# Last gate's list scatters bound one by one to TensorE's products, and two W1 pieces of the second early slot loaded and rounded during the first one

## The chip, the cores and the metric

The kernel runs on one core of one Trainium2 chip. The metric is device time in microseconds (us) of one execution. TensorE (PE) does the matrix products, and PEld is its weight load, which overlaps them; VectorE (DVE) and ScalarE (ACT) do elementwise work and empty the accumulators; GpSimd (POOL) does some copies and issues the indirect transfers; SyncE (SP) issues the plain ones. Each engine takes its own instructions strictly in order.

## The reference

A linear attention with exponential features is followed by a mixture of experts with one expert a token. A token may keep the expert of the token before it, so its expert is known only after a scan over the sequence.

```python
# attention: 8 batches, 8 heads, 576 tokens, head size 64, 128 features
proj = x @ w_phi;  proj -= max(|proj|);  phi = [exp(proj), exp(-proj)]     # for q and for k
out  = (phi_q @ (phi_k.T @ v)) / (phi_q @ sum(phi_k) + 1e-6)
# experts: E = 8, D = 512, F = 1024
logits = x @ w_gate;  local = sigmoid(x @ w_local)
e[s] = argmax(logits[s]) if s == 0 or local[s] < 0.5 else e[s-1]
y[s] = softmax(logits[s])[e[s]] * (relu(x[s] @ w1[e[s]]) @ w2[e[s]])
```

## The kernel before

**Front.** Two batches make a batch pair (NBP = 4) of 9 chunks (NC = 9) of 128 tokens. `step` handles two chunks: projections (L351), transposes (L371), the sums over keys (L403, L416), and the quotients of earlier chunks (L483). A step takes some 3.7 us on every engine. Attention rows go to `xs` in HBM, gate values to `lg` on POOL (L511 to L514).

**Gates.** After each batch pair, `gate` (a Python generator, advanced step by step) finds each token's expert and its place in the expert's list. Its chain runs DVE, PE, DVE, PE: `g_code`, a transpose (L738), a scan, `g_dg`, a small product (L750), `g_mk`, `g_cm`, `g_ci`, `g_ef`, a transpose (L767), `g_oh`, `g_ohb`, ten counting products (L780 to L785), `g_rk`, and `ri`, the row numbers. Then nine scatters (L836), one a chunk, write token number and probability into the list `lst` in HBM. The gates of pairs 0 to 2 run as `background` work, one stretch a step through `chores`; that of the last pair (`last_gate`) runs while the first products of the experts are already under way (`self.tail`).

**Early slots.** After gate 1 enough is known to choose two slots of 3 x 128 tokens of one expert (`eslots`), which can be computed before the last gate is through. `plan_early` fetches their lists (L902, read back through a transpose, L933) and `early_chores` gathers their tokens (L1223) and loads and rounds the eight weight pieces of the first slot, four of W1 and four of W2.

**Main slots.** `plan_main` needs the last gate's counts (product L942). Some 110 small DVE instructions give `p_rih` and `p_rim`, the rows of the lists to fetch; the fetches (L902, on POOL) wait until all scatters have landed. A list comes back by the transposes at L933, into `p_tokm`, and then the tokens are gathered (L1223).

**One slot.** `layer1` makes eight blocks f of hidden units, 12 products each (L1305 to L1307: a value is kept as a high and a low part, whi/wlo for weights, xhi/xlo for tokens, hh/hl for hidden values). ACT writes hh (L1358), DVE hl (L1359). `layer2` makes for each 128 tokens (a unit) eight steps f of three products, then y (L1415), and POOL scatters y to the output (L1419). `pause()` in `layer1` and the test on f in `layer2` run one entry of the list `between`: 16 places in `layer1`, two a block.

**Weights.** A piece is 512 KB. `load` has SP fetch it into one of three `wraw` buffers; `split` has ACT round it to whi (L1170) and DVE subtract for wlo (L1173), which frees the buffer. `spare()` splits the pieces beyond the newest two and loads one more; `used` calls it. So the second slot's first three pieces are fetched early, and its fourth waits until the first is split.

**What orders the work.** The code's order, run through a scheduler that may interleave each engine's instructions; a few explicit orders: `issue_after` and `here()` (behind the last product, on the issuing side), `behind_it` (a real wait on another engine's semaphore). `slots(eslots, soon, later)` takes what to run in the places of `layer1` (`soon[i]`) and `layer2` (`later[i]`) of slot i; `go` advances the last gate by one stretch.

Of the kernel before, what the change touches and what calls it, by code (L numbers as in the profile page):

```python
# [39 lines left out]
QUOTA = 16  # L40
LINE = 256

STEP = "step"

# [35 lines left out]
class Kernel:  # L82
# [9 lines left out]
    def run(self):  # L92
        nc, tc, A = self.nc, self.tc, self.A
        act, dve = self.act, self.dve
        with ExitStack() as root:
# [38 lines left out]
            n = NBP * NHP * NC  # L134
# [36 lines left out]
            plan = self.plan_main()  # L171
            go = self.advance

            def rest():
                for _ in self.last_gate:
                    if self.ranked is not None:
                        for x in self.background:
                            for _ in x:
                                pass

            def listed():
                next(plan)
                next(plan)

            def read():
# [2 lines left out]
            no = lambda: None  # L188
            m = []
# [13 lines left out]
            def singles():  # L203
                more()
                m[0]()
            self.slots(self.eslots, soon=[[no, no, no, go, no, no, go, no, no, go, rest],
                                          [no] * 9 + [read, a[0], a[1], no, a[2], no, a[3]]],
                       later=[[listed], [no, no, singles] + [lambda k=k: m[k]() for k in (1, 2, 3)] + [more]])
            back.close()
            self.mid.close()  # L210
            self.open_rest(root)
# [36 lines left out]
    def table(self):  # L248
# [8 lines left out]
        def by_three(o, x, n):  # L257
            dve.tensor_scalar(o, x, 3.0, None, ALU.is_ge)
            for k in range(2, n):
                dve.scalar_tensor_tensor(o, x, 3.0 * k, o, ALU.is_ge, ALU.add)  # L260
        yield STEP
        with self.tc.issue_after(self.last_dve.ins):
            by_three(eth, u, EARLY)
            dve.scalar_tensor_tensor(erest, eth, -3.0, u, ALU.mult, ALU.add)
        yield STEP
        with self.tc.issue_after(self.last_dve.ins):
            dve.tensor_scalar(c[11], u, 2.0, None, ALU.mult)
            dve.tensor_scalar(c[12], u, 2.0, 1.0, ALU.mult, ALU.add)
        yield STEP
        with self.tc.issue_after(self.last_dve.ins):  # L270
# [428 lines left out]
    def gate(self, bp):  # L699
# [79 lines left out]
        with self.here():  # L779
            pe.matmul(t4, self.triu, ohb, start=True, stop=False)  # L780
            for c in range(NC - 1):
                k = NC - 1 - c
# [40 lines left out]
        tc.keep_in_program_order(dve.tensor_copy(pr[:, :, 0], self.tokid[:, bp * NC:bp * NC + NC]))  # L823
        dve.tensor_mul(pr[:, :, 1], se, su)
        self.scattering = True
        for c in range(NC):
            yield STEP
            while self.tail and not self.drained:
                yield STEP
            if self.tail and self.ranked is None:  # L830
                self.late += 1
                while self.late > ROW and self.ranked is None:
                    self.held_back = True
                    yield STEP
            with self.paced():
                ins = pool.indirect_dma_start(self.lst[:, :], bass.IndirectOffsetOnAxis(ri[:, c:c + 1], 0),  # L836
                                              pr[:, c, :], None)
            if self.late > ROW:
                self.behind_it(ins, self.ranked, "it would hold the last gate's chain")
            tc.declare_no_dep(ins.ins, group="scatter", reason="scattered rows are distinct")  # L840
            tc.add_to_no_dep_group("scatter", ins.ins)
            self.scattered.append(ins)
# [543 lines left out]
    def layer2(self, s, between, held=None):  # L1386
        tc, dve, pool = self.tc, self.dve, self.pool
        hh, hl = s["h"]
        self.need(s, 8) if len(s["ei"]) == 1 else None
        for k in range(s["n"]):  # L1390
            if hasattr(self, "psr"):
                t = self.psr.tile([128, DM], F32, name="l2")
            else:
                t = self.psb.tile([128, DM], F32, name="l2", tag="nm")
            m = min(128, s.get("cols", s["n"] * 128) - k * 128)
            o = slice(k * 128, k * 128 + m)
            for f in range(8):
                c = slice((f % 2) * DM, (f % 2) * DM + DM)
                self.both(s, 4 + f // 2, t[0:m], hh[:, f, o], hl[:, f, o], c, f == 0, f == 7)
                if f in ((0, 2) if s["n"] > 1 else (1, 3, 5)) and between:  # L1400
                    between.pop(0)()
                if f % 2 and k == s["n"] - 1:
                    self.used(1)
                elif f % 2:
                    self.spare()
            last = held is not None and k == s["n"] - 1
            y = self.mx2.tile([128, DM], F32, name="yl", bufs=1) if last else self.mx2.tile([128, DM], F32, name="y")
            u = s["u"] + k
            if last:
                w = s["prob"][0:m, u:u + 1]  # L1410
                self.act.activation(y[0:m], t[0:m], AF.Copy, scale=w)
            elif hasattr(self, "psr"):
                self.marks[dve] = dve.tensor_scalar_mul(y[0:m], t[0:m], s["prob"][0:m, u:u + 1])  # L1413
            else:
                self.marks[self.act] = self.act.activation(y[0:m], t[0:m], AF.Copy, scale=s["prob"][0:m, u:u + 1])  # L1415
                self.last_y = self.marks[self.act]

            def put(y=y[0:m], at=s["tok"][0:m, u:u + 1]):
                ins = pool.indirect_dma_start(self.A["out"], bass.IndirectOffsetOnAxis(at, 0), y, None,  # L1419
                                              bounds_check=NT - 1, oob_is_err=False)  # L1420
                tc.declare_no_dep(ins.ins, group="outs", reason="each token is written once")
                tc.add_to_no_dep_group("outs", ins.ins)
            if last:
                held.append(put)
            else:
                put()

    def slots(self, order, held=None, soon=(), later=()):
# [19 lines left out]
        for i, s in enumerate(order):  # L1448
            while s.get("asked", len(s.get("w", ()))) < 8:
                self.spare()  # L1450
            self.need(s, 4)
            new = order[i + 1] if i + 1 < len(order) else None
            rows = self.tokens(ahead[i], bool(soon) and i == 0, self.last_y if held is not None and i == 0 else None)
            first, rest = list(soon[i]) if i < len(soon) else [], rows
            if not soon and s["n"] > 1:
                some = [f for u in rows for f in u[0:3]]
                first = [lambda: None] * 16
                for k, f in enumerate(some):
                    first[1 + k * 15 // len(some)] = f
                rest = [u[3] for u in rows]  # L1460
            if not soon:
                rest += [lambda x=x, k=k: self.gather_x(x, k) for x in ahead[i + 1] for k in range(x["n"])]
            if len(s["ei"]) == 1:
                self.layer1(s, first)
            else:
                self.layer1_two(s, [])
            if i < len(later):
                rest = list(later[i]) + rest
            self.layer2(s, rest, None if new else held)
            for f in rest:  # L1470
                f()
            s.clear()
# [131 lines left out]
```

## Time and profile before

| | |
|---|---|
| median of 3 runs | 715.51 us (713.83 to 719.53) |
| the profiled execution | 712.14 us, of which span 710.3 us |
| PE busy | 698.4 us, 98% of the span |
| PEld busy | 617.9 us, 87% |
| DVE / ACT / POOL busy | 460.7 / 411.8 / 265.0 us |
| granted TensorE clock, mean | 0.997 |
| mean DMA traffic | 176 GB/s |

The span is the time from the first to the last instruction of the profiled execution; 1.9 us lie around it. Busy times are averages over stages: the front (to 276 us), the first early slot (276 to 312 us), the second (312 to 348 us) and the main slots (from 348 us). In a timeline row the figures are start, duration, engine, line, operation, and in brackets how long the engine was idle before it and what released it.

### The profile page before, as it was taken

How to read it: one execution, taken by the hardware profiler on the slowest of the kernel's cores; microseconds unless marked ns; L12 is line 12 of the kernel's file. 1: busy time of each engine (PE TensorE's matmuls, PEld its weight loads, DVE VectorE, ACT ScalarE, POOL GpSimd, SP SyncE). 2: the span in 40 equal slices, each digit the busy share in tenths (PEclk: the TensorE clock that was granted, in tenths of full speed). 3: DMA queues.
4: the chain of work that ended last, by engine and by line, in shares of the span. 5: the costliest groups of instructions: out<-in, count | busy, mean ns of one | idle time of the engine just before them, and what ended most of it. 6: DMA issues, size and time to landing. Idle time of an engine off the chain costs nothing. (4 is left out here: it accounts for less than half of the span.)

```text
span 710.3 us, 22974 instructions
## 1 busy us (share of the span) xinstructions
PE 698.4 (98%) x9576; PEld 617.9 (87%) x9576; DVE 460.7 (65%) x876; ACT 411.8 (58%) x888; POOL 265.0 (37%) x532
## 2 busy tenths in 40 slices
PE   7999999999999999999999999999999999999996
PEld 6999999999999999888887986889888877888985
DVE  6898899889998995683537446535643367554522
ACT  5777776777768873434465654745754269471512
POOL 0211101430146675562345551345744236443311
PEclk9999999999999999999999999999999999999998
DMA  7855545555466863254818975344886375444200
GB/s 232 268 154 148 160 124 155 148 149 161 134 183 198 252 189 113 64 181 129 280 70 294 405 279 194 135 149 150 265 307 252 110 243 172 150 163 155 76 27 31
DMA packets 66074, 125.17 MB, mean 176 GB/s; under 512 B 7180, under 2 KB 45260, under 8 KB 65910
## 3 DMA queue, kind: packets, MB, share of 16 engines
q1 hardware_dynamic: 57680, 100.90, 44.8%
q0 software_dynamic: 7968, 22.58, 9.0%
q8 instruction: 76, 1.25, 0.7%
q14 instruction: 30, 0.25, 0.1%
q10 hardware_dynamic: 320, 0.20, 0.1%
HBM read 102.11 MB, written 21.80 MB: 174 GB/s over the span
## 5 line engine op out<-in xcount | busy, mean ns | idle before, releaser
L1173 DVE TENSOR_TENSOR wlo<-wraw,whi 128x1024 fp32r<-128x1024 f32 x80 | 96.4, 1222 | 37.8 <-ACT whi L1170 37.5
L1305 PE MATMUL l<-whi,hh 128*128 128x512 f32 (+1 forms) x288 | 113.4, 394 | 0.5 <-ACT hh L1358 0.5
L1306 PE MATMUL l<-wlo,hh 128*128 128x512 f32 (+1 forms) x288 | 112.7, 391 | 0.8 <-DVE wlo L1173 0.8
L1307 PE MATMUL l<-whi,hl 128*128 128x512 f32 (+1 forms) x288 | 112.6, 391 | 0.0
L362 ACT ACTIVATE kp<-sb 128x512 f32<-128x512 f32 x144 | 83.3, 623 | 48.9 <-DVE sb L359 48.1
L1359 DVE SCALAR_TENSOR_TENSOR hl<-l,hh 128x512 fp32r<-128x512 f32 (+3 forms) x84 | 50.4, 600 | 93.2 <-ACT hh L1358 93.1
L1170 ACT CAST whi<-wraw 128x1024 fp32r<-128x1024 f32 x80 | 82.4, 1047 | 43.8 <-PE l L1307 27.0
L1358 ACT ACTIVATE hh<-l 128x512 fp32r<-128x512 f32 (+3 forms) x84 | 44.0, 525 | 108.9 <-PE l L1307 57.2
L1305 PE MATMUL l<-xhi,whi 128*128 128x384 f32 (+4 forms) x308 | 106.8, 347 | 0.0
L1307 PE MATMUL l<-xhi,wlo 128*128 128x384 f32 (+4 forms) x308 | 106.5, 346 | 0.0
L1306 PE MATMUL l<-xlo,whi 128*128 128x384 f32 (+4 forms) x308 | 106.4, 345 | 0.0
L358 DVE TENSOR_REDUCE m<-pj 128x8 f32<-128x1024 f32 (+1 forms) x74 | 88.3, 1193 | 20.4 <-PE pj L351 18.3
L1285 POOL COPY xg<-z 32x128 f32<-32x128 f32 x208 | 70.4, 339 | 58.7 <-DVE z L1273 41.4
L359 DVE TENSOR_TENSOR sb<-pj,m 128x1024 f32<-128x1024 f32 (+1 forms) x74 | 88.5, 1196 | 5.6
L351 PE MATMUL pj<-first,kq 64*128 64x128 f32 x1152 | 85.3, 289 | 3.5 <-DMA first<-in_first 3.4
L483 PE MATMUL nm<-kvs,qp 128*64 128x73 f32 x2304 | 86.3, 227 | 0.5 <-issue 0.4
L1419 POOL DMA_INDIRECT out<-y,p_tokm x31 | 37.4, 1205 | 127.2 <-DVE y L1413 126.0
L386 ACT ACTIVATE qp<-pj 128x512 f32<-128x512 f32 x144 | 78.1, 596 | 8.4 <-PE pj L371 7.5
L483 PEld LDWEIGHTS nm<-kvs,qp 128*64 128x64 f32 x2304 | 79.1, 137 | 1.0 <-issue 0.7
L351 PEld LDWEIGHTS pj<-first,kq 64*128 64x128 f32 x1152 | 71.4, 190 | 9.4 <-DMA first<-in_first 3.4
L403 PE MATMUL kvp<-v,kp 128*64 128x65 f32 x2048 | 75.3, 224 | 0.1
L1285 ACT COPY xg<-z 32x128 f32<-32x128 f32 x208 | 61.7, 296 | 20.3 <-DVE z L1273 16.0
(266 smaller groups left out, 1080.0 us busy)
## 6 DMA issues: line engine op xcount, KB each, us to landing
wraw<-in_w1h SPq DMA_DIRECT2D x44, 512.0 KB, 5.1
wraw<-in_w2h SPq DMA_DIRECT2D x44, 512.0 KB, 5.6
kq<-in_kqT SPq DMA_DIRECT2D x47, 384.0 KB, 4.1
v<-in_va SPq DMA_DIRECT2D x48, 195.0 KB, 3.5
xs<-xo SPq DMA_DIRECT2D x48, 128.0 KB, 2.4
whi<-in_w1h SPq DMA_DIRECT2D x8, 512.0 KB, 5.8
wlo<-in_w1h SPq DMA_DIRECT2D x8, 512.0 KB, 8.6
whi<-in_w2h SPq DMA_DIRECT2D x8, 512.0 KB, 7.2
```

The lines of the kernel that those rows point to most:

```text
L351: self.last_pe = self.pe.matmul((q if j else t)[:, h, i % 2, j, :], kq[r, j, s], self.w2[r], start=True, stop=True)
L358: dve.tensor_reduce(m[:, a:a + n], x[:, s], AX.X, ALU.max, apply_absolute_value=True)
L359: self.last_dve = dve.tensor_sub(to[:, s], x[:, s], m[:, a:a + n].unsqueeze(2).broadcast_to([128, n, 128]))
L362: self.last_act = act.activation(kp[:, :, :, sg, :].rearrange("p c h f -> p h c f"), sb[:, :, :, 0], AF.Exp, scale=1.0 - 2 * sg)
L386: self.act.activation(qp[:, sg].rearrange("p h (c r k) -> p (h c) r k", c=2, r=2), src, AF.Exp, scale=1.0 - 2 * sg)
L483: self.last_num = self.pe.matmul(e["t"][r, c - c0, k], self.ch[i]["qp"][:, sg, h, q0 + r.start:q0 + r.stop], kvs[:, sg, k], start=sg == 0, ...
L1170: self.act.copy(hi, raw)
L1173: (low or self.dve).tensor_sub(lo[:, c], raw[:, c], hi.bitcast(F32)[:, c])
L1285: self.marks[engine] = copy(to[q, :, g], z[g, :, b, :])
L1305: mm(o, ah, bh, start=first, stop=False)
L1306: mm(o, ah, bl, start=False, stop=False)
L1307: self.last_pe = mm(o, al, bh, start=False, stop=last)
```

## The change

In this section and in the prediction c0 to c8 are the nine scatters of the last gate.

- `gate` yields a new mark `LIST` ahead of the last gate's scatters. In the front, gates 0 to 2 issue two scatters a step and not one.
- `rest`, which ran the remainder of the last gate and all open scatters in one go in the 11th place of the first early slot's `layer1`, is replaced by `row`: one stretch or one scatter a call. Six calls stand in the last six places of that `layer1` (from block 5 on), five more in its `layer2`: `row` is called in unit 0 at f = 0 (`plan_row`), 4, 6 and in unit 1 at f = 4, 6. Five scatters of gate 2 that are still open at the end of the front run freely as before.
- Each of c0 to c8 waits for PE's last product as of its place (`behind_it(ins, self.last_pe, ...)`).
- The first two places of `layer1` call `spare` (load a piece), and the sixth `landed(1)`: the first two W1 pieces of the second early slot are split there, behind block 2, and not after block 7.
- In the front the order moves as well: on PE the early lists' transposes (L933) stand four steps earlier, and gate 2's L750, L767 and L780 one step earlier each, so that they follow its L738 step by step, as those of gates 0 and 1 do.
- `layer2` of the first early slot has places at f = 0, 2, 4, 6 (before: 0, 2). The plan's first part stands where it was; its second part, the fetches, is called (`listed`) after unit 1 and not together with the first.

```diff
-STEP = "step"
+STEP, LIST = "step", "list"
...
-            def rest():
-                for _ in self.last_gate:
-                    if self.ranked is not None:
-                        for x in self.background:
-                            for _ in x:
-                                pass
+            def lists():
+                for x in self.last_gate:
+                    if x is LIST:
+                        break
+                for x in self.background + [self.last_gate]:
+                    for _ in x:
+                        yield
+            flow = lists()
+
+            def row():
+                next(flow, None)
+
+            def plan_row():
+                next(plan)
+                row()
 
             def listed():
-                next(plan)
+                for _ in flow:
+                    pass
                 next(plan)
...
-            self.slots(self.eslots, soon=[[no, no, no, go, no, no, go, no, no, go, rest],
+            self.slots(self.eslots, soon=[[self.spare, self.spare, no, go, no, lambda: self.landed(1), go, no, no, go] + [row] * 6,
                                           [no] * 9 + [read, a[0], a[1], no, a[2], no, a[3]]],
-                       later=[[listed], [no, no, singles] + [lambda k=k: m[k]() for k in (1, 2, 3)] + [more]])
+                       later=[[plan_row, 0, row, row, 1, 2, row, row, listed], [no, no, singles] + [lambda k=k: m[k]() for k in (1, 2, 3)] + [more]])
...
+        if self.tail:
+            yield LIST
         for c in range(NC):
-            yield STEP
+            if self.tail or c % 2 == 0:
+                yield STEP
...
+            if self.ranked is not None:
+                self.behind_it(ins, self.last_pe, "the list's rows are written one transfer after the other")
...
-                if f in ((0, 2) if s["n"] > 1 else (1, 3, 5)) and between:
+                if f in ((1, 3, 5) if s["n"] == 1 else (0, 2, 4, 6) if s is self.eslots[0] else (0, 2)) and between:
...
-                rest = list(later[i]) + rest
+                rest = [x if callable(x) else rest[x] for x in later[i]]
```

What stands on DVE in the middle of the last gate's chain, between `g_cm` and `g_ef`, during the first early slot's `layer1`, before:

```order
L78 TENSOR_REDUCE g_cm<-g_mk 9x1
L78 TENSOR_SCALAR g_ci<-g_sc,g_cm 9x128
L78 TENSOR_SCALAR g_ci<-g_ci 9x128
L78 CAST g_ef<-g_ci 9x128
L1359 SCALAR_TENSOR_TENSOR hl<-l_6342,hh 128x384
```

And now (the line numbers are those of the changed file; wlo is at L1188, hl at L1374):

```order
L78 TENSOR_REDUCE g_cm<-g_mk 9x1
L1188 TENSOR_TENSOR wlo<-wraw,whi 128x1024 x2
L78 TENSOR_SCALAR g_ci<-g_sc,g_cm 9x128
L1374 SCALAR_TENSOR_TENSOR hl<-l_6363,hh 128x384
L78 TENSOR_SCALAR g_ci<-g_ci 9x128
L78 CAST g_ef<-g_ci 9x128
L1374 SCALAR_TENSOR_TENSOR hl<-l_6391,hh 128x384
```

The two subtractions of the moved pieces and one hl come ahead of `g_ef`; on ACT their two roundings stand between the hh of blocks 2 and 3.

The place on PE where `g_ef` is read (`pt<-first,g_ef`), between blocks 4 and 5 of the same `layer1`, before:

```order
L1307 MATMUL l_6370<-xhi,wlo 128x384
L767 MATMUL pt<-first,g_ef 128x9
L1305 MATMUL l_6393<-xhi,whi 128x384
L1306 MATMUL l_6393<-xlo,whi 128x384
L1307 MATMUL l_6393<-xhi,wlo 128x384
```

And now:

```order
L1322 MATMUL l_6391<-xhi,wlo 128x384
L1320 MATMUL l_6414<-xhi,whi 128x384
L1321 MATMUL l_6414<-xlo,whi 128x384
L1322 MATMUL l_6414<-xhi,wlo 128x384
L1320 MATMUL l_6414<-xhi,whi 128x384
L1321 MATMUL l_6414<-xlo,whi 128x384
L777 MATMUL pt<-first,g_ef 128x9
L1322 MATMUL l_6414<-xhi,wlo 128x384
```

The transpose has moved five products back; the counting products that follow it stand three products later than before. Nothing else differs on PE from there to the end of the program.

POOL's queue from the first early slot's `layer1` to the fetch of the main list (`lr<-lst,p_rim`), before (`p_rih` are two small fetches of half lists):

```order
L836 DMA lst<-pr,ri 36992x16 x17
L1419 DMA out<-y,p_toke 4608x512
L902 DMA lr<-lst,p_rih_6651 4x1024
L902 DMA lr<-lst,p_rih_6669 4x1024
L1419 DMA out<-y,p_toke 4608x512 x2
L902 DMA lr<-lst,p_rim 30x2048
```

And now:

```order
L849 DMA lst<-pr,ri 36992x16 x13
L1434 DMA out<-y,p_toke 4608x512
L849 DMA lst<-pr,ri 36992x16
L917 DMA lr<-lst,p_rih_6762 4x1024
L1434 DMA out<-y,p_toke 4608x512
L917 DMA lr<-lst,p_rih_6780 4x1024
L917 DMA lr<-lst,p_rim 30x2048
L1434 DMA out<-y,p_toke 4608x512
```

Three scatters have gone to the front; the output of unit 0 now stands ahead of the last scatter, and the main fetch ahead of the output of unit 2.

## Rows read from the trace of the kernel before

**Rows 1.** The page, busy time of PE: us, share of the span, instructions

```profile
PE 698.4 (98%) x9576; PEld 617.9 (87%) x9576; DVE 460.7 (65%) x876; ACT 411.8 (58%) x888; POOL 265.0 (37%) x532
```

**Rows 2.** What PE waited for: us in total, times, longest

```profile
PE pj L351 <- DMA first<-in_first: 3.4, 1, 3.4
PE l L1306 <- DVE wlo L1173: 0.8, 1, 0.8
PE l L1305 <- ACT hh L1358: 0.5, 1, 0.5
```

**Rows 3.** Stretches: us, busy (instructions) of PE, PEld, DVE, ACT, POOL; clock; DMA share, GB/s

```profile
275.87:293.84 17.97, 17.97 (x112) 17.16 (x111) 10.56 (x43) 3.60 (x8) 9.03 (x13) 1.00 0.09 23
293.84:312.00 18.16, 18.16 (x87) 14.73 (x86) 17.04 (x92) 9.28 (x12) 14.81 (x12) 1.00 0.47 142
312.00:329.80 17.80, 17.80 (x102) 17.42 (x101) 7.05 (x33) 4.42 (x10) 6.23 (x7) 1.00 0.40 129
```

**Rows 4.** Timeline of DVE: gate 1, last gate, then split and plan (start, duration)

```profile
176.64 0.21 DVE L78 CAST g_ef<-g_ci 9x128 f32<-9x128 int32 x1
...
283.90 0.15 DVE L78 TENSOR_REDUCE g_cm<-g_mk 9x1 f32<-9x9 f32 x1
284.64 0.22 DVE L78 CAST g_ef<-g_ci 9x128 f32<-9x128 int32 x1
285.49 0.56 DVE L1359 SCALAR_TENSOR_TENSOR hl<-l,hh 128x384 fp32r<-128x384 f32 x1 [0.63 <-ACT hh L1358]
...
295.50 1.23 DVE L1173 TENSOR_TENSOR wlo<-wraw,whi 128x1024 fp32r<-128x1024 f32 x1
296.79 1.21 DVE L1173 TENSOR_TENSOR wlo<-wraw,whi 128x1024 fp32r<-128x1024 f32 x1
...
314.90 0.14 DVE L78 TENSOR_SCALAR p_rim<-p_rowm 54x1 int32<-54x1 f32 x1
```

**Rows 5.** Timeline of PE: gate 1; last gate; last scatter's product; list read

```profile
176.91 0.22 PE L767 MATMUL pj<-first,g_ef 9*128 9x9 f32 x1
...
286.95 0.22 PE L767 MATMUL pt<-first,g_ef 9*128 9x9 f32 x1
288.62 0.21 PE L780 MATMUL pt<-g_ohb,consts 128*128 128x72 bf16 x1
...
304.27 0.39 PE L1307 MATMUL l<-whi,hl 128*128 128x512 f32 x1
...
322.52 0.41 PE L933 MATMUL pt<-first,lr 34*128 34x34 f32 x2
```

**Rows 6.** Timeline of ACT: hh of block 2; two roundings in a row

```profile
282.54 0.49 ACT L1358 ACTIVATE hh<-l 128x384 fp32r<-128x384 f32 x1 [1.71 <-PE l L1307]
...
294.43 1.98 ACT L1170 CAST whi<-wraw 128x1024 fp32r<-128x1024 f32 x2
```

**Rows 7.** Timeline of SP: issue of the second early slot's second W1 piece

```profile
265.12 0.35 SPq L1157 DMA_DIRECT2D wraw<-in_w1h  x1
```

**Rows 8.** The page, DMA issues: count, KB each, median us to landing

```profile
wraw<-in_w1h SPq DMA_DIRECT2D x44, 512.0 KB, 5.1
```

**Rows 9.** Timeline of POOL: scatters, an output, fetches

```profile
289.61 0.96 POOL L836 DMA_INDIRECT lst<-pr,ri  x1 [5.42 <-DVE pr L78]
...
304.19 0.96 POOL L836 DMA_INDIRECT lst<-pr,ri  x1 [0.31 <-DMA lst<-pr,ri]
305.45 3.55 POOL L1419 DMA_INDIRECT out<-y,p_toke  x1 [0.30 <-issue]
310.52 1.86 POOL L902 DMA_INDIRECT lr<-lst,p_rih  x1 [0.31 <-issue]
316.32 0.92 POOL L902 DMA_INDIRECT lr<-lst,p_rim  x1 [0.31 <-issue]
```

**Rows 10.** Tile lst, its transfers (scatters among them)

```profile
DMA to landing us min/median/max: 2.1/3.6/5.3
```

**Rows 11.** Tile lr, its transfers (the fetched lists)

```profile
DMA to landing us min/median/max: 4.0/5.0/5.3
```

## The prediction, made before the changed kernel ran

> **What bounds the kernel now.** I read the page's busy times first: PE works 98% of the span [rows 1]. Then what PE waited for. The reader is to see how little there is: 3.4 us for the first inputs, before any work, 0.8 us for one wlo and 0.5 us for one hh, both in main slots [rows 2]. None of the three waits lies in the two early slots, which the change rearranges. Then the stretches: in the first slot's layer 1 (275.87 to 293.84), its layer 2 (to 312.00) and the second slot's layer 1 (to 329.80) PE is busy in every microsecond, at a granted clock of 1.00 [rows 3]. So in the region of the change an edit can gain nothing unless it shortens PE's own work, and PE has the same products in both programs. It can lose, wherever something PE reads comes later than PE does.
>
> [...]
>
> **The change, part by part.**
>
> *Front: two scatters a step, gate 2's chain a step earlier.* The same 36 scatters are issued, three more of them ahead of the early slots; POOL is busy 37% [rows 1]. On PE gate 2's L750, L767 and L780 now follow L738 in consecutive steps, and on DVE `g_mk` to `g_ef` interleave with rc and xo. This is how gates 0 and 1 stand in the kernel before. Gate 1 prices it: `g_ef` ends at 176.64 + 0.21 = 176.85 and L767 starts at 176.91 [rows 4, 5]; it fits by 0.06 us, and PE's list has no wait there. Cost 0; as upper bound, one further short DVE instruction in the way, 0.2 us.
>
> *Two pieces split in the first slot's layer 1.* The second piece is issued by SP at 265.12 [rows 7] and lands some 5.1 us later [rows 8], at 270, so the data are there. ACT: hh of block 2 ends at 282.54 + 0.49 = 283.03, the two roundings take 1.98 us [rows 6] and end at 285.0. DVE: the first wlo can start when the first rounding ends, 284.05, which is also when `g_cm` ends (283.90 + 0.15); the second starts 1.29 later and takes 1.21 [rows 4], so DVE is back at the gate's chain at 284.05 + 1.29 + 1.21 = 286.55. From `g_cm`'s end to `g_ef`'s end it took 284.86 - 284.05 = 0.81 before; now one hl (0.56 [rows 4]) stands in between: `g_ef` ends at 286.55 + 0.81 + 0.56 = 287.92 if nothing overlaps, at 287.4 if hl hides in the chain's own latencies. PE reads it at L767: before at 286.95 [rows 5]; now five products later, 5 x 0.175 = 0.87, at 287.82. A tie: between 0.4 us early and 0.1 late. Before, `g_ef` was 2.1 us early: that cover is used up, and every further 0.1 us on DVE is 0.1 us of PE. I take 0.1; as upper bound hl once more, 0.7. The counting products stand 3 products later than before, 288.62 + 0.52 = 289.14, 1.32 behind L767 where there were 1.67 [rows 5]; but the hl that stood between `g_oh` and `g_ohb` now precedes them, which gives 0.56 back against 0.35. Cost 0.
>
> What the moved split frees: the fourth and fifth pieces can be fetched from about 286 and not 297 (the first wlo of before starts at 295.50), in a stretch where the DMA engines are 9% busy [rows 3]. The list of waits shows no PE wait for these pieces, so no gain. DVE has two wlo (2 x 1.21) fewer between counts and `p_rim`, which so comes at about 314.90 + 0.14 - 2.4 = 312.6.
>
> *Scatters bound to PE.* Before, POOL sat idle 5.42 us until the last gate's DVE chain released it at 289.61 [rows 9]. That chain moves with L780 by 0.5 us, and one hl (0.56) now stands ahead of `ri`: c0 leaves at about 290.7, say 291. Scatters follow every 1.27 us at POOL's own pace (0.96 and 0.31 of idle [rows 9]), so c7 leaves at 291 + 7 x 1.27 = 299.9, and each of c0 to c7 later than the product it waits for: the binding decides nothing for them. The output of unit 0 comes next, at 299.9 + 1.27 = 301.2, and is done by 302 or, at the longest one seen (3.55 [rows 9]), by 305. c8 waits for the third product of unit 1, f = 4, which ends at 304.27 + 0.39 = 304.66 [rows 5]. So c8 leaves at 304.7, half a microsecond after the last scatter of before (304.19 [rows 9]). That is where the binding decides, and the only place.
>
> Behind c8 on POOL: the two half-list fetches with the output of unit 1 between them, then the main fetch. c8 lands 3.6 us after issue [rows 10], 308.3; fetch 0.92, output about 1, fetch 0.92 with 0.3 between [rows 9] end at 312.0; then `p_rim`: the main fetch leaves at 312.6 and not at 316.32 [rows 9], and lands 5.0 us later [rows 11] at 317.6. PE reads it at 322.52 [rows 5]: 4.9 us early, where it was 1.2 us early before (316.32 + 5.0 = 321.3). Cost 0, gain 0, but a wider margin.
>
> One row speaks for the slower end: outputs and fetches took 3.55 and 1.86 us on POOL at 305.45 and 310.52 [rows 9], against 0.92 at 316.32. [...]
>
> *Extra places, `plan_row`, `listed` apart from it.* No instruction is added to PE; the plan's DVE instructions are the same. Cost 0.
>
> **Sum.** 0 to 0.1 + 0.1 + 0 = +0.1 us on the profiled execution: 712.14 to 712.2. The median of before lies 3.4 us above its profiled execution (715.51); the forecast is for the median: **715.5 us**.
>
> **Rivals.**
> 1. *The runs that aren't profiled lose what the profile shows as a thin margin.* The list was only 1.2 us early, and the executions spread over 713.83 to 719.53. If the 3.4 us between profile and median are PE waiting at L933 for a late list, the wider margin gives them back: 715.5 - 3.4 = 712.1. For it: the margin. Against: nothing in the trace shows such a wait. 12%.
> 2. *The bound scatters make the list late (slower).* c8 waits behind PE and the output ahead of it, and what follows takes its longest times: c8 at 305.1 (301.2 + 3.55 + 0.3), landing 5.3 [rows 10] at 310.4, then fetch 1.86, output 3.55, fetch 1.86 and three gaps of 0.3: main fetch at 318.6, landing 5.3 [rows 11] at 323.9. PE waits 1.4 us at L933: 716.9. It decides from the moment the main fetch leaves later than 322.5 - 5.3 = 317.2. To pass 1% it would have to leave 7.2 us later than that. 8%.
> 3. *DVE reaches `g_ef` late*, up to 0.7 us: 716.2. It is the tie above, at its far end. 12%; it is within the same verdict.
> 4. *The change does not do what it says*: the binding only forbids what POOL's pace forbids anyway. Then nothing moves but the wlo pair: 715.5, the same time as the forecast; counted with it.
>
> **How the numbers follow.** The forecast (nothing but PE's tie, at most +0.1) has 65%, rivals 1, 2 and 3 have 12, 8 and 12%, and 3% are left for what I don't see. A measurement of this kernel can tell about 1% (7.2 us) from no change; all named cases lie within that. The range takes rival 1 at its low end (712.1, less half a microsecond: 711.5) and, at the high end, the highest run of before (719.53), since rivals 2 and 3 add only 1.4 us to the median and single runs scatter by more: 711.5 to 719.5. Faster by over 1% would need 7.2 us out of PE waits that total under 6 in the whole profile: 2%. Slower by over 1%: 4%. Within 1%: 94%.
>
> **What would show it.** In the profile after: PE's waits in the main slots are still some 0.8 us for a wlo and 0.5 us for an hh; L767 of the last gate starts within 0.3 us of `g_ef`'s end; c0 to c7 follow each other at 1.27 us, and only c8 waits for PE; the main fetch leaves near 312.6. Rival 2 shows as a PE wait at L933 for `lr`, rival 3 as one at L767 for `g_ef`. The prediction would be wrong if PE shows a new wait of several microseconds in the two early slots, or if the main slots, whose order is the same, lose or gain time.

## The result, and the profile after

The changed kernel took 721.83 us (median of 14 runs, 719.60 to 725.84) and the kernel before, beside it, 717.37 (14 runs, 713.83 to 721.14): ratio 1.0064, 95% interval 1.0048 to 1.0081, 4.5 us slower. Forecast were 715.5 us, in a range of 711.5 to 719.5, and no change. Of the 6.3 us by which that was missed, 1.9 lie in the kernel before, which took 717.37 us here and 715.51 in the three runs that the forecast started from; 4.5 lie in the change. The profiled execution of the changed kernel took 721.97 us, of which span 720.1, at a mean granted clock of 0.999.

One thing has to be known to read the numbers below. The effect found here depends on the measurement, not on the program alone: of the measurements in which the changed kernel or its decisive part ran, three show it (the first sort) and two don't (the second), whole sets of runs at a time, and one chip showed it once and on another occasion, by the time of the kernel before (the pairs themselves did not run there), was of the second sort. Each comparison is therefore made within one measurement, whose kernel before is named with it; A is the one above, B to G follow.

The page, busy time of the engines (answers to [rows 1]), and PE's waits, longest first (answers to [rows 2]):

```profile
PE 704.3 (98%) x9576; PEld 620.9 (86%) x9576; DVE 460.5 (64%) x876; ACT 411.8 (57%) x888; POOL 263.6 (37%) x535
```

```profile
PE pj L361 <- DMA first<-in_first: 3.4, 1, 3.4
PE kvp L413 <- issue: 1.5, 5, 0.4
PE l L1320 <- ACT hh L1373: 1.1, 1, 1.1
PE pj L381 <- issue: 0.8, 2, 0.4
PE l L1321 <- DVE wlo L1188: 0.8, 1, 0.8
PE pj L469 <- issue: 0.5, 1, 0.5
PE pj L361 <- issue: 0.5, 2, 0.3
```

New are the lines with "issue": PE stood still although nothing that the profile shows was missing. They lie at L361, L381, L413 and L469, which are lines of the front (L351, L371, L403 and L459 before). The share of busy time, 98% in both programs, hides them. The lines name some 3.3 us of standing still; PE's busy time grew by 5.9 us besides, for the same 9576 products. The ends of products are modelled, so that a part of each stop is booked as work: 32 products at L413 that take 1.15 us without a stop (trace of D below) stand here as 0.52 us for 9 and 0.86 for 22.

Where the time goes: line up the two programs product by product and read how much later each starts. At 126 us the changed kernel is 0.3 us late, after gate 0's pairs of scatters (144.3 us) 3.3, after gate 1's (218 us) 7.5, after gate 2's two pairs (277 us) 9.1, and behind the last gate's rearrangement (289.5 us) 9.2; at 363 us it is still 9.2. So the part that the prediction worked out at length cost nothing, and the part that it priced at nothing cost nearly everything. (The two profiled executions stand 9.8 us apart, the medians 4.5: the one of before, 712.14, is quicker than every run of before in this measurement.)

The front at close range, in stretches of 4 us (behind the length: busy us and instructions of PE, PEld, DVE, ACT and POOL, then granted clock, DMA share, GB/s). Before:

```profile
130.00:134.00 4.00, 4.00 (x114) 3.85 (x112) 3.77 (x6) 2.72 (x7) 1.68 (x4) 1.00 0.64 188
134.00:138.00 4.00, 4.00 (x115) 3.85 (x112) 3.32 (x7) 3.32 (x9) 1.69 (x5) 1.00 0.45 128
```

After:

```profile
130.00:134.00 4.00, 3.59 (x88) 3.34 (x88) 2.85 (x5) 1.85 (x4) 2.39 (x7) 1.00 0.51 154
134.00:138.00 4.00, 3.76 (x92) 3.51 (x90) 3.07 (x5) 2.42 (x8) 2.59 (x6) 1.00 0.49 135
```

PE gets through 180 products where it did 229. Timeline of POOL in the changed kernel, two steps, scatters only:

```profile
128.00 1.07 POOL L849 DMA_INDIRECT lst<-pr,ri  x1 [0.69 <-issue]
...
129.44 1.02 POOL L849 DMA_INDIRECT lst<-pr,ri  x1 [0.17 <-issue]
...
132.54 1.00 POOL L849 DMA_INDIRECT lst<-pr,ri  x1
...
133.90 0.98 POOL L849 DMA_INDIRECT lst<-pr,ri  x1 [0.16 <-issue]
```

Timeline of PE beside it, the sums over keys only:

```profile
129.90 0.52 PE L413 MATMUL kvp<-v,kp 128*64 128x65 f32 x9
130.82 0.86 PE L413 MATMUL kvp<-v,kp 128*64 128x65 f32 x22 [0.41 <-issue]
...
134.27 0.76 PE L413 MATMUL kvp<-v,kp 128*64 128x65 f32 x11
135.28 0.84 PE L413 MATMUL kvp<-v,kp 128*64 128x65 f32 x21 [0.24 <-issue]
```

The second scatter runs from 129.44 to 130.46, PE goes dry after its ninth product and resumes at 130.82; the next one runs from 133.90 to 134.88, PE goes dry after the eleventh and resumes at 135.28. PE comes back some 0.4 us behind the end of the second scatter, in the middle of a series, at no border of a tile; no operand can have been what it waited for: kp was written 1.19 us before the product at 130.82 began, and 0.62 us before the one at 135.28. Behind the first scatter of a step there is no stop.

### The profile page after: what moved, and what is told of

Read it like the earlier page. It is cut to its first block, busy times and chain, and to the rows that moved or that the text cites. A ratio compares the mean times of both kernels' runs of the same rounds, so it can differ in the third digit from the quotient of the medians.

```text
span 720.1 us, 22985 instructions
## 1 busy us (share of the span) xinstructions
PE 704.3 (98%) x9576; PEld 620.9 (86%) x9576; DVE 460.5 (64%) x876; ACT 411.8 (57%) x888; POOL 263.6 (37%) x535
## 5 line engine op out<-in xcount | busy, mean ns | idle before, releaser
L1188 DVE TENSOR_TENSOR wlo<-wraw,whi 128x1024 fp32r<-128x1024 f32 x80 | 96.2, 1221 | 38.4 <-ACT whi L1185 37.7
L1374 DVE SCALAR_TENSOR_TENSOR hl<-l,hh 128x512 fp32r<-128x512 f32 (+3 forms) x84 | 50.4, 600 | 93.5 <-ACT hh L1373 91.8
L361 PE MATMUL pj<-first,kq 64*128 64x128 f32 x1152 | 86.4, 289 | 4.0 <-DMA first<-in_first 3.4
L361 PEld LDWEIGHTS pj<-first,kq 64*128 64x128 f32 x1152 | 72.1, 191 | 10.2 <-DMA first<-in_first 3.4
L413 PE MATMUL kvp<-v,kp 128*64 128x65 f32 x2048 | 78.2, 225 | 1.9 <-issue 1.5
```

The source lines that it names most:

```text
L361: self.last_pe = self.pe.matmul((q if j else t)[:, h, i % 2, j, :], kq[r, j, s], self.w2[r], start=True, stop=True)
L1188: (low or self.dve).tensor_sub(lo[:, c], raw[:, c], hi.bitcast(F32)[:, c])
```

## Experiments

**B. The parts, each alone** (kernel before: 712.72 us in this measurement). `e1_one_a_step` is the changed kernel without the pairs, `e2_pairs_only` the kernel before with the pairs and nothing else:

```diff
 e1   for c in range(NC):
-         if self.tail or c % 2 == 0:
-             yield STEP
+         yield STEP
 e2   for c in range(NC):
-         yield STEP
+         if self.tail or c % 2 == 0:
+             yield STEP
```

> The changed kernel with one scatter a step in the front, as before; the moved split of the two W1 pieces and the binding of the last gate's scatters stay. Theory A (the loss sits in the front's steps with two scatters, 12 such steps by some 0.65 us of stopped PE in the profile): ratio to the kernel before 0.998 to 1.002, and in its trace no PE idle put down to issue between 125 and 265 us. Theory B (the loss comes from the early slots, where the split moved and the scatters were bound): ratio 1.005 to 1.008, as with the whole change.

> The kernel before with one edit alone: two scatters a step in the front, one right behind the other. Theory A: all of the loss is back, ratio 1.004 to 1.009, with PE idle put down to issue in the steps with two scatters (12 of them). Theory B: ratio 0.998 to 1.002.

Measured: 712.84 us, ratio 1.0002 (0.9988 to 1.0016), and 713.14 us, 1.0006 (0.9989 to 1.0022). The rest is free, as expected, but so were the pairs, which theory A put at 1.004 to 1.009. In the trace of the pairs the second scatters follow as closely as in the changed kernel (130.02 behind 128.58) and PE doesn't stop. Theory A fell in this form, for this measurement. (The pairs in the front are ten, not twelve as expected: five of gate 2's scatters stay behind for the early slots.)

`e3_pairs_spaced` lets the second scatter of a step wait for the step's first kp, which sets seven of the ten pairs apart (the first pair and gate 2's two stay 1.4 us from start to start); `e4_pool_busy` puts POOL arithmetic behind each single scatter of the kernel before:

```diff
 e3   with self.paced(late=c % 2 == 1):      # tick reads kp instead of m
 e4   ins = pool.indirect_dma_start(self.lst[:, :], ...)
+     if not self.tail:
+         x = self.w2[:, 0:116].unsqueeze(1).broadcast_to([128, 3, 116])
+         with tc.issue_after(ins.ins):
+             pool.tensor_add(w, x, x)
```

> The changed kernel, still two scatters in a step of the front, but the second one is released by the step's first kp (ACT) and not by m (DVE): it leaves some 1.9 us behind the first, with about 0.8 us of free time on POOL between them, where the pair had 0.35. Theory A1 (PE is stopped because the second scatter follows the first too closely): most of the loss goes, ratio 0.998 to 1.003, PE idle by issue at most 1 us in the front. Theory A2 (what counts is how many list rows are written in a step): the loss stays, ratio 1.004 to 1.008. Theory A3 (a scatter that runs into the products of 64 or 128 columns stops PE wherever it stands): the loss stays or grows.

> The kernel before, one scatter a step, and right behind each of the 27 scatters of the front one POOL addition of 128x348 elements (about 1 us, no transfer; its result is read by nobody). Theory A4 (the issuing of descriptors by a second scatter stops PE): nothing, ratio 0.998 to 1.002. Theory A5 (POOL at work in SBUF for some 2 us on end stops PE, whatever the work): 27 stops of some 0.6 us, 16 us, ratio 1.015 to 1.025.

Measured: 1.0000 (0.9983 to 1.0017), and 714.71 us, 1.0035 (1.0017 to 1.0052). The first tells nothing where pairs are free anyway. Of the 27 additions expected, 19 run in the front, as eight of gate 2's scatters are issued behind it. 2.0 us for 19 additions of 0.78 us, 0.10 each, is no stop of 0.6 us; by the trace gate 0's nine cost nothing, and the loss lies in gate 1's stretch. But as pairs were free here, it tells only that the additions themselves are nearly so.

**C. The changed kernel again, and larger doses** (kernel before: 715.72 us). `e5_extra_scatter` puts a second scatter of the same rows behind each one that runs in the front, into a list that nobody reads (19 of them, not 27 as expected); `e6_nine_in_a_step` is the changed kernel with a gate's nine scatters in one step:

```diff
 e5   ins = pool.indirect_dma_start(self.lst[:, :], ...)
+     if not self.tail:
+         with tc.issue_after(ins.ins):
+             more = pool.indirect_dma_start(self.lst2[:, :], ...)
 e6   for c in range(NC):
-         if self.tail or c % 2 == 0:
+         if self.tail or c == 0:
              yield STEP
```

> The changed kernel itself, once more. The pairs alone cost nothing (1.0006) and neither does the rest alone (1.0002). Theory P (the two parts together cost it, though each alone is free): ratio 1.004 to 1.009 and PE idle by issue in the steps with two scatters, 0.2 to 0.5 us each. Theory C (the stopped PE belongs to the loading and the chip of that measurement, not to the program): ratio 0.998 to 1.002, no PE idle by issue in those steps.

> The kernel before, and behind each of the 27 scatters of the front a second one of the same 128 rows into a list that nobody reads. If two scatters on end stop PE, there are now 27 such places in 27 steps: at 0.65 us each 17.5 us, ratio 1.02 to 1.03. If two on end are free, as the pairs alone were: 0.998 to 1.003.

> The changed kernel with all nine scatters of a gate in one step of the front, some 12 us of POOL on end. If PE is stopped while a second and later scatter is issued: 8 stops a gate, 24 in all, 0.65 to 1.3 us each, 16 to 31 us, ratio 1.022 to 1.044. If scatters on end are free for PE: only the additions to lg stand behind them on POOL, and xo's buffers come free late; ratio 1.000 to 1.010.

Measured: 722.76 us, 1.0107 (1.0085 to 1.0129); 733.56 us, 1.0244 (1.0225 to 1.0263); 747.69 us, 1.0431 (1.0409 to 1.0453). Here the stops are back, and they grow with the dose. By the first one's expectation, that spoke for theory P; its ratio lies even above the 1.004 to 1.009 named for it. Ten pairs cost 7.04 us, 0.70 each; 19 extra scatters 17.84, 0.94 each. That 17.5 had been expected is no support for 0.65 us a pair: it came of 27 scatters, and the agreement is chance. With nine on end each of the 24 further ones costs 31.97 / 24 = 1.33 us. Nine on end, in stretches of 3 us (behind the length: PE, PEld, DVE, ACT and POOL, busy us and instructions; granted clock, DMA share, GB/s):

```profile
127.00:130.00 3.00, 3.00 (x86) 2.85 (x86) 2.67 (x5) 2.17 (x7) 1.66 (x4) 1.00 0.54 159
130.00:133.00 3.00, 1.84 (x33) 1.39 (x29) 0.00 (x0) 0.31 (x1) 2.55 (x5) 1.00 0.23 70
133.00:136.00 3.00, 1.31 (x14) 0.70 (x14) 2.45 (x2) 0.00 (x0) 2.67 (x5) 1.00 0.46 134
136.00:139.00 3.00, 0.84 (x6) 0.63 (x6) 0.00 (x0) 2.39 (x5) 2.67 (x5) 0.54 0.05 11
```

And PE's timeline in it, where the scatters follow every 1.34 us:

```profile
131.53 0.36 PE L413 MATMUL kvp<-v,kp 128*64 128x65 f32 x5 [0.43 <-issue]
132.28 0.39 PE L413 MATMUL kvp<-v,kp 128*64 128x65 f32 x5 [0.39 <-issue]
133.02 0.38 PE L413 MATMUL kvp<-v,kp 128*64 128x65 f32 x5 [0.36 <-issue]
133.77 0.35 PE L413 MATMUL kvp<-v,kp 128*64 128x65 f32 x4 [0.37 <-issue]
```

PE advances by four or five products at a time, then has nothing. From 86 products in 3 us it comes down to 33, 14 and 6, and DVE and ACT, which work on what it makes, are busy in one of these three stretches each (but for 0.31 us). So PE goes on, at 53 products in 9 us, and the price of 1.33 us for a scatter every 1.34 us holds more than these stops. Among it are the products that follow the fall of the granted clock, to 0.54 in the last of these stretches and to 0.50 in the next (139 to 142 us): 16 of them take 1.16 us at a granted clock of 1.00 (L361, row of 129.12 in the same trace) and 2.08 behind that stretch:

```profile
143.52 2.08 PE L361 MATMUL pj<-first,kq 64*128 64x128 f32 x16
```

**D. All on one chip** (kernel before: 712.88 us), to tell a matter of the measurement from a joint effect of the two parts:

> The changed kernel again, beside its parts on the same chip. Theory C (whether a second scatter on end stops PE is a matter of the chip or of how the program was loaded): either all kernels with pairs are slower together, 1.004 to 1.012, or none is, 0.998 to 1.002. Theory P (the pairs cost only together with the rest of the change): this one 1.004 to 1.012, the pairs alone 0.998 to 1.002.

> Pairs alone, on the same chip as the changed kernel. Theory C: the same ratio as the changed kernel within 0.003. Theory P: 0.998 to 1.002 whatever the changed kernel shows.

> The pair with its second scatter released by kp. Where the changed kernel is slower by 0.4% or more: if the short distance is what stops PE, 0.998 to 1.003; if it is the second scatter as such, the changed kernel's ratio within 0.003. Where the changed kernel is not slower: 0.998 to 1.002, and nothing is told.

> One scatter a step with the rest of the change. By either theory 0.998 to 1.002; if the moved split or the binding costs something that the first chip hid, 1.003 or more.

Measured: 0.9998 (0.9982 to 1.0013), 1.0005 (0.9988 to 1.0021), 1.0012 (0.9997 to 1.0028), 1.0000 (0.9985 to 1.0015). None is slower, the whole change included. That speaks for theory C and against P, by which the whole change is slower wherever it runs. The same two steps in the changed kernel here, POOL's scatters:

```profile
129.63 1.07 POOL L849 DMA_INDIRECT lst<-pr,ri  x1 [0.69 <-issue]
...
131.07 1.02 POOL L849 DMA_INDIRECT lst<-pr,ri  x1 [0.17 <-issue]
...
132.92 1.00 POOL L849 DMA_INDIRECT lst<-pr,ri  x1
...
134.28 0.98 POOL L849 DMA_INDIRECT lst<-pr,ri  x1 [0.16 <-issue]
```

and PE's sums over keys:

```profile
131.52 1.15 PE L413 MATMUL kvp<-v,kp 128*64 128x65 f32 x32
...
135.21 1.13 PE L413 MATMUL kvp<-v,kp 128*64 128x65 f32 x32
```

The same program, the same scatters at the same distance and of the same length, and 32 products in one piece. Lined up with C's trace of the same program, C falls back by 0.8 to 1.3 us in each of the ten steps with a pair, 9.5 us, and by 0.6 us in all the time between; that is about the difference of the two medians, 722.76 and 712.77. A's trace, lined up with D's, falls back by 8.4 us in the ten steps. The kernel before stands 2.8 us higher in C as well, which is why C's ratio shows 7.0 us and not 10: the ratios, 0.45 to 0.70 us a pair, understate what a pair costs PE.

**E. Pairs alone and the rest alone where pairs stop PE** (kernel before: 716.05 us; nine in a step beside them show the stops):

> Pairs alone, on another chip. If this chip is of the kind on which scatters on end stop PE (nine in a step near 1.043 beside this run): 1.004 to 1.011, all of the change's loss, and PE idle by issue in the steps with two scatters. If the loss needs the rest of the change as well: 0.998 to 1.002 even there. On a chip of the other kind: 0.998 to 1.002.

> The rest of the change alone, one scatter a step. If the pairs are all of the loss: 0.998 to 1.002 on either kind of chip. If the moved split or the binding has a share in it: 1.003 to 1.008 on a chip on which nine in a step are slow.

> Nine scatters in one step, with the changed kernel's rest. On a chip on which scatters on end stop PE: 1.035 to 1.045, as before. On one of the other kind: 1.000 to 1.005 if it does not feel them at all; 1.010 to 1.030 if it only has a larger reserve, which two on end do not use up and nine do.

Measured: pairs alone 722.50 us, 1.0093 (1.0076 to 1.0109); the rest alone 713.05 us, 0.9955 (0.9939 to 0.9971); nine in a step 745.49 us, 1.0418 (1.0399 to 1.0436). This settles the part: ten pairs cost 6.45 us, 0.65 each, and the rest costs nothing; it came out 3.0 us quicker, below the 0.998 to 1.002 expected. Lined up with the trace of pairs alone in D, this one falls back by 8.6 us in the ten steps. By theory P the pairs alone would have been free, so P falls here. The trace of the pairs shows the stops at the same places:

```profile
129.50 0.48 PE L403 MATMUL kvp<-v,kp 128*64 128x65 f32 x8
130.35 0.88 PE L403 MATMUL kvp<-v,kp 128*64 128x65 f32 x23 [0.36 <-issue]
```

and the trace of the rest alone has no idle time by issue at all between 125 and 225 us, where the kernels with pairs have 2.7, 3.3 and 2.6 us in A, C and E (no kernel has more than 0.2 us there in the other measurements). That holds for the scatters into the list alone. Between 225 and 275 us, where gathers and subtractions on POOL stand beside them, traces of either sort with one or two scatters a step have idle time by issue as well, up to 1.3 us (spaced pairs in D, 229.76 us), and the profile of before has 0.29 us at 266.59 us beside a single scatter. What causes these is not shown.

**F and G. What is left** (kernel before: 713.01 and 712.81 us). `e7_rest_unbound` is one scatter a step with the rest of the change, without the line that binds c0 to c8 to a product:

```diff
-     if self.ranked is not None:
-         self.behind_it(ins, self.last_pe, ...)
```

> The kernel before, for its profile on this chip. Ratio 0.998 to 1.002. On a chip of the first kind (median near 716): its trace shows some 3 us of PE idle put down to issue that the profile of before shown here (712.14) does not have, either beside single scatters and fetches in the front (before 265 us) or in the two early slots. On the other kind (median near 712.8): nothing new.

> One scatter a step, the moved split and the later list as in the rest of the change, but no scatter bound to a product of PE: the last gate's scatters leave at POOL's own pace. On a chip of the first kind: 0.994 to 0.997 if the moved split gains the 3 us, 0.999 to 1.002 if the binding gains them. On the other kind: 0.998 to 1.002.

> The changed kernel with the second scatter of a step released by kp, some 0.8 us of free time on POOL between the two. On a chip of the first kind (kernel before near 716): if the short distance stops PE, the time of one scatter a step, 0.994 to 1.001, and no PE idle by issue at the second scatters; if two in a step are too many wherever they stand, 1.006 to 1.012. On the other kind (before near 713): 0.998 to 1.002.

> One scatter a step with the rest of the change. On a chip of the first kind: 0.994 to 0.997 if the gain seen there once is the program's, 0.998 to 1.002 if it was chance. On the other kind: 0.998 to 1.002.

Measured in F: the kernel before against itself 0.9976 (0.9954 to 0.9997), without the binding 1.0003 (0.9986 to 1.0020). In G, on the chip of E: spaced pairs 1.0003 (0.9989 to 1.0018), one a step 1.0000 (0.9984 to 1.0017). By the kernel before, near 713 us, both are of the sort of B and D, so neither question of them was answered: the spaced pair was never measured where close pairs stop PE, and the 0.9955 of the rest alone was not seen again (1.0002, 1.0000 and 1.0000 in the other three). A kernel that came out at 0.9976 against itself, below the 0.998 expected, says what a quarter of a per cent is worth here.

## Why the prediction was wrong, step by step

**The step that failed** is "Front: two scatters a step, gate 2's chain a step earlier", its "Cost 0; as upper bound, one further short DVE instruction in the way, 0.2 us". Measured: 4.5 us in A, 7.0 in C and, for the pairs alone, 6.45 in E, at 0.45 to 0.70 us a pair against the kernel before, and 0.6 to 1.3 us a pair where two traces are lined up; and nothing in B and D. The wait that the upper bound had in view, PE behind gate 2's `g_ef`, came at 0.4 us in C (L777) and 0.5 in E (L767) and not at all in A: twice the bound, and still a small part. It failed in its reasoning and not only in its size. The cover named was POOL's 37% of busy time, a share of the span, which says that POOL has room and nothing of what a POOL instruction does to PE meanwhile. The price was taken from gate 1's chain on DVE [rows 4, 5], which is another question. No row of the trace had two scatters on end beside products that take 0.035 us each (32 in 1.13 us), so by the prediction's own rule the cost was unknown, and neither bound was worked out from a row of a scatter.

**What the trace could not have told.** The profile of before was of an execution of 712.14 us, below the lowest of its own three runs (713.83). The prediction saw the 3.4 us between that and the median, and made a rival of it. Measurements in which pairs stop PE have the kernel before at 717.4, 715.7 and 716.1 us, the others at 712.7 to 713.0: by its time the profile belongs to the second sort, where pairs are free.

A second sign says the same, and it needs no pairs. A trace also records when semaphores change. Of the changes that engines make while POOL issues an indirect transfer, 19 to 30% are missing in each of the seven traces of A, C and E, that of the rest alone (75 of 359), where PE does not stop, among them, and 1 to 3% in the other thirteen, the profile of before included (8 of 387). So the condition belongs to the measurement and is there with one scatter a step too. Whether the recording has a part in stopping PE, or only loses records for the same reason, was not tested.

What costs the kernel before, which has no pairs, those 3 us isn't shown: no profile of it from a measurement of the first sort exists. The nearest is the trace of `e5_extra_scatter` in C, which has its order in the early slots, with twelve scatters on end from 306.57 to 322.10 us. There PE stops by issue and then waits for hl and for the list (L940 is L933 of before):

```profile
PE l L1312 <- DVE hl L1366: 1.0, 1, 1.0
PE pt L940 <- DMA lr<-lst,p_rim: 0.5, 1, 0.5
PE l L1312 <- issue: 0.4, 1, 0.4
```

Lined up with the trace of the kernel before in F, it falls back by 2.9 us between 320 and 343 us, near the 2.8 us by which the kernel before is slower in C. Scatters bound one by one never stood more than seven on end (the rest alone in E), which would fit that run's gain of 3.0 us. This is argued from one trace, not shown.

**The split of two pieces in the first slot: right.** Counting the 9.2 us by which all is later here, `g_ef` was to end at 296.6 to 297.1 and L777 (L767 before) to start at 297.0 (five products later, at 0.175 us a product, that is 17.80 us for 102 in [rows 3]). DVE's timeline, then PE's:

```profile
296.42 0.22 DVE L78 CAST g_ef<-g_ci 9x128 f32<-9x128 int32 x1
```

```profile
296.98 0.22 PE L777 MATMUL pt<-first,g_ef 9*128 9x9 f32 x1
```

`g_ef` ends at 296.64, 0.3 us ahead: the early end of the tie. The stretches that answer to [rows 3] show PE busy throughout, the middle one, cut to the same 18.16 us, with the same 87 products:

```profile
284.91:302.91 18.00, 18.00 (x114) 17.11 (x112) 12.68 (x46) 5.48 (x10) 7.45 (x11) 1.00 0.26 81
302.91:321.07 18.16, 18.16 (x87) 14.76 (x86) 15.77 (x97) 7.40 (x10) 12.05 (x12) 1.00 0.38 121
```

**The binding: right in cost, wrong in one detail.** "The binding decides nothing for them" was said of c0 to c7. POOL's timeline (c0, c3, c7, the output, c8, the main fetch; answers to [rows 9]):

```profile
300.94 0.97 POOL L849 DMA_INDIRECT lst<-pr,ri  x1 [7.56 <-PE l L1321]
...
304.77 1.98 POOL L849 DMA_INDIRECT lst<-pr,ri  x1 [0.30 <-issue]
...
310.89 0.97 POOL L849 DMA_INDIRECT lst<-pr,ri  x1 [0.30 <-PE tr L1267]
312.17 1.01 POOL L1434 DMA_INDIRECT out<-y,p_toke  x1 [0.30 <-issue]
314.48 0.97 POOL L849 DMA_INDIRECT lst<-pr,ri  x1 [1.30 <-DMA lst<-pr,ri]
...
323.40 0.92 POOL L917 DMA_INDIRECT lr<-lst,p_rim  x1 [1.89 <-DVE p_r L934]
```

c0 waited for PE and left at 300.94, 0.7 us later than forecast (291 + 9.2 = 300.2); one scatter took 1.98 us and not 0.96, so c7 left at 310.89 and not 309.1; c8 at 314.48 (forecast 313.9), the main fetch at 323.40 (321.8). (What the row of c8 names as ending its wait is the landing of an earlier scatter; in D's trace it is the product.) The scatter of 1.98 us ran while DVE worked on two wlo (1.23 us from 304.68 us, 1.21 from 305.96), and so did the output of 3.55 us (three wlo, 304.47 to 308.10) and the fetch of 1.86 us (one, from 310.38) in [rows 9]. Of the 117 indirect transfers of the profile after, 20 of the 35 that overlap a wlo of DVE took over 1.3 us, and none of the other 82. PE reads the list at 331.7, so by the transfer time of [rows 11] it was still some 3 us early. PE does not wait at L948 (L933 before): cost 0, the second rival did not come about. Of the places for it the prediction was right also in that c8 comes late and harms nothing; without any binding the time is the same (1.0003).

**The other rivals.** The third (DVE late at `g_ef`) did not happen in the early slot. The first (a gain of 3.4 us) appears once, as the rest alone in E (3.0 us), and in none of three repetitions, all of them where the kernel before takes 713 us. The wait that it named exists, but is small: 0.5 us at L940 in the trace of `e5_extra_scatter`, 0.2 us at L933 in that of the kernel before in F, none in the profile of before. That the list's wider margin is what gained is not shown. The slower side had a rival, but the wrong one: it sat on the last gate, where all the working had gone.

**What the stop is** can be said only in part. Shown: in the front it came with a second indirect transfer on POOL close behind a first (0.35 us between them), and with one list scatter a step not; it falls on PE alone and not at an operand, it grows with the number of scatters on end, and POOL's work as such isn't the cause, as beside POOL's four wlo subtractions (2.79 us from 276.88 us) PE was busy for 2.69 us and no stop by issue began, in the very profile of A. Whether the short distance is what counts is not shown, as spaced pairs never ran where close ones stop PE. Few scatters on end in the early slot cost nothing either, five in A (287.29 to 293.39 us) and nine with the pairs alone in E; PE's products there take 0.17 us, five times those of the front, and in A it was busy for all of those 6.10 us. Twelve on end did stop it there (the trace of `e5_extra_scatter` above). That PE lives on some reserve meanwhile is a conjecture of the author's, and no run shows it; shown is, in A, that a first scatter of 1.07 us left PE without a stop and a second of 1.02 us, 0.37 us behind it, did not. Why some measurements show no stop at all stays open: the durations of the scatters, the distance between them and PE's own products are the same in both, and so is the duration of the transfers of the queue that the page calls instruction (q8: 0.99 us in the median in C's trace of the changed kernel, 0.98 in D's).

## What to carry to other kernels

An engine with room is no cover: ask of each work that is moved closer together what the engine that sets the time does meanwhile, above all where that engine lives on very short instructions (here pairs stopped PE at 0.035 us a product, and five scatters on end did not at 0.17), and where no row has the two side by side, call the price unknown. Indirect transfers issued by POOL are better spread than issued in pairs (between 125 and 225 us, one list scatter a step of 3.6 us left PE at most 0.2 us idle by issue in any trace), and one scatter a step with the rest of this change was in no measurement slower than the kernel before. A profiled execution that is quicker than every run beside it describes another condition than the one that is timed; and a part that measures as free has to be measured again beside the whole.

## What was not expected of the hardware

- Two indirect transfers 0.35 us apart on POOL can cost PE 0.45 to 0.70 us by the medians of ten pairs, 0.94 us by those of 19, and 0.6 to 1.3 us a pair by the traces; nine on end cost 1.2 to 1.3 us for each further one, the fall of the granted clock to 0.50 included.
- The same program shows this in some measurements and not in others, and the kernel before moves with it, 716 to 717 against 713 us; one chip had the kernel before at 716.05 in E and at 712.81 in G. The traces of A, C and E lack 19 to 30% of the semaphore changes made while POOL issues an indirect transfer, the others 1 to 3%.
- In the stretch with nine scatters on end PE was busy for 1.84 and 1.31 of 3 us, and its granted clock then fell from 1.00 to 0.54 in the mean of the next 3 us and to 0.50 in the 3 us after them; the products that followed were slower too (16 at L361 in 2.08 us and not 1.16).
